# Transposing the normalised q through the DMA crossbar instead of on TensorE, in a fused linear attention and gated scan kernel

## Chip, cores, metric

One core of one Trainium2 chip. The metric is the device time of the kernel in microseconds (us). The kernel before takes 152.72 us (median of 2 runs, 152.36 to 153.08). All verdicts use runs in the fast state. By rule, a difference under 2% counts as the same; where the text calls a smaller one real, its 95% interval leaves out 1.

Names as the profile has them: PE is TensorE (matmuls), DVE the vector engine, ACT the scalar engine, POOL the GpSimd engine, SP the engine that issues the DMAs (copies between memories, done by 16 DMA engines). A lower-case name with an arrow, such as eqT<-eq, is a buffer written from another.

## The reference, cut

```python
def _attn_ref(q, k, v):                       # 8 batches, 8 heads, 576 positions, 64 wide
    q_s = np.exp(q - q.max(-1, keepdims=True)); q_s /= q_s.sum(-1, keepdims=True) + 1e-9
    k_s = np.exp(k - k.max(2, keepdims=True));  k_s /= k_s.sum(2, keepdims=True) + 1e-9
    kv = np.einsum('bhsd,bhse->bhde', k_s, v)
    return np.einsum('bhsd,bhde->bhse', q_s, kv)
# the heads side by side are x (8, 576, 512); then
    proj = x @ w_in                            # 512 -> 1024: val, gate
    h = a[0, 0] * h + val[:, t, :]             # a scan over t, kept as ys
    return (silu(gate) * ys) @ w_out           # 512 -> 512, float32
```

## The kernel before

It works on 8 batches (attention) and 9 chunks of 512 rows (projections, scan, output). Per batch: exp of q (ACT), row sums (DVE), the normalising multiplication (POOL, "norm"), exp of k (ACT), a cast of v (POOL), kv on TensorE, q transposed, xt = kv by transposed q on TensorE, and its eviction into xT (ACT). Per chunk: val and gate (TensorE), scan and gate multiplication (DVE), tanh (ACT), z (POOL), outp (TensorE), its eviction and the store.

All instructions of all engines are put in one order by a small list scheduler in the kernel. It has a cost for each operation, a "due" time for each, and rings of buffers; at each step an engine takes the operation of smallest due time among those that could start. Each engine then works strictly in this order. All DMAs are issued from SP.

```python
RINGS = {"qf": 2, "kf": 2, "vf": 2, "eq": 2, "ek": 1, "vb": 1, "eqT": 2, "kvc": 2, "y": 12,
    "th": 4, "u": 4, "z": 4, "ob": 3, "tp": 1, "ax": 1, "pp": 3, "po": 2, "qs": 3, "axp": 2, "xT": 4}
...
        def load(x, b, q2):
            ...
            nc.sync.dma_start(out=t[:, h], in_=r[:, h])          # 1152 KB: one of q, k, v of a batch
        def transp(self, e, b, g):                                # g = 0, 1, 2: 18 transposes per batch
            tp = buf("tp", (b, g))
            src = buf("eq", b).rearrange("p q c h d -> p (q c) (h d)")
            for j in range(6):
                nc.tensor.transpose(tp[:, j, :], src[:, 6 * g + j, :], ident)
        def tevac(self, e, b, g):                                 # PSUM -> SBUF on DVE or ACT
            copy(e, buf("eqT", b).rearrange("p q c h r -> p (q c) (h r)")[:, 6 * g:6 * g + 6, :],
                 buf("tp", (b, g)))
        def xt(self, e, b, q2, hf):
            xp, kvc, eqT = self._xp(b, 2 * q2 + hf), buf("kvc", b), buf("eqT", b)
            ...                                                   # rhs=eqT[r, q2, :, h2, ...]
    def idle(name, key, n):                                       # filler matmuls for the clock
        ...
        for _ in range(n):
            nc.tensor.matmul(dst, lhsT=ident, rhs=zero, start=True, stop=True)
```

The softmax here doesn't subtract the row's maximum and nothing guards it: scores larger than these inputs give would overflow.

Of the kernel before, what the change touches and what calls it, by code (L numbers as in the profile page):

```python
# [13 lines left out]
PSUM = bass.MemoryType.PSUM  # L14
# [10 lines left out]
    "cwin": {"DVE": 0.4, "POOL": 0.62, "ACT": 0.6},  # L25
# [3 lines left out]
PERIOD = 21.61  # L29
LOOK = 0.02  # L30
WARM = [0.0, 0.0]
DUE_W, DUE_CW = [-109.79, 225.14], [-179.42, 203.56]
DUE_WO, DUE_CWO, DUE_D = 501.34, -557.67, [-146.47, 373.31]
DUE = {"lq": -20.7, "lk": -40.61, "lv": -135.24, "expq": 201.96, "qsum": 161.83,
    "norm": -295.36, "expk": 15.63, "vcast": -104.69, "kv": -278.49, "transp": -215.75,
    "tevac": -180.01, "kvn": -413.4, "xt": -313.37, "xevac": -104.58, "val": -182.38,
    "scan": 210.04, "gate": -266.21, "tanh": -98.69, "gmul": -92.36, "zmul": -112.88,
    "outp": 179.81, "oevac": 92.95, "store": 182.18}
DUE_B = {
    0: {"expq": 70.47, "qsum": -5.23, "norm": 6.74, "expk": 90.41, "vcast": 61.5, "kv": 75.48,  # L40
        "transp": -244.47, "tevac": 224.73, "kvn": 118.97, "xt": -443.24, "xevac": -113.28,
        "lq": -296.19, "lk": -144.58, "lv": -63.26},
    1: {"expq": 139.16, "qsum": -170.8, "norm": -52.54, "expk": 148.63, "vcast": -144.79,
        "kv": 33.35, "tevac": -19.3, "kvn": -231.76, "xt": -7.07, "xevac": 61.09, "lq": -161.43,
        "lk": 13.79, "lv": 6.2},
}
DUE_C = {
    0: {"val": -128.64, "scan": 153.13, "gate": -14.99, "tanh": 40.59, "gmul": 85.28,
        "zmul": 191.57, "outp": -110.65, "oevac": -99.93, "store": 54.59},
    1: {"val": -73.24, "scan": -9.07, "gate": 15.05, "tanh": -32.83, "gmul": 0.37,  # L50
        "zmul": -152.72, "outp": 24.34, "oevac": -105.03, "store": -137.19},
    7: {"val": -26.9, "scan": 78.94, "gate": -10.0, "tanh": -19.5, "gmul": 166.0, "zmul": 77.14,
        "outp": -9.86, "oevac": 136.84, "store": 72.5},
    8: {"val": -5.34, "scan": 160.56, "gate": 161.01, "tanh": 107.09, "gmul": 129.49,
        "zmul": 330.75, "outp": 83.16, "oevac": 59.02, "store": -116.2},
# [3 lines left out]
       "tevac": ["DVE", "DVE", "DVE", "DVE", "DVE", "ACT"],  # L59
       "xevac": ["ACT"],  # L60
       "oevac": ["ACT", "ACT", "ACT", "DVE"],
       "norm0": ["DVE", "POOL"],
       "norm1": ["DVE", "POOL"],
       "vcast0": ["POOL", "ACT", "DVE", "POOL"],
       "xevac0": ["ACT", "DVE", "DVE", "ACT"],
       "cwin": ["ACT", "DVE", "POOL", "ACT"]}
RINGS = {"qf": 2, "kf": 2, "vf": 2, "eq": 2, "ek": 1, "vb": 1, "eqT": 2, "kvc": 2, "y": 12,
    "th": 4, "u": 4, "z": 4, "ob": 3, "tp": 1, "ax": 1, "pp": 3, "po": 2, "qs": 3, "axp": 2,
# [3 lines left out]
def operations(B, NCH, NM):  # L72
# [10 lines left out]
    for kt in range(4):  # L83
        for h in range(2):
            d = DUE_W[h] + 0.1 * kt
# [15 lines left out]
    for b in range(B):  # L101
        due = {n: PERIOD * b + x + DUE_B.get(b, {}).get(n, 0.0) for n, x in DUE.items()}
        first = b == 0
# [29 lines left out]
        for g in range(3):  # L133
            a("transp", "PE", 0.35, due["transp"] + 0.5 * g, (b, g),
              reads=[("n", b, x) for x in ((0,), (0, 1), (1,))[g]], writes=[("t", b, g)],
              uses=[("eq", b), ("tp", (b, g))])
            e, c = pick("tevac", 3 * b + g)
            a("tevac", e, c, due["tevac"] + 0.5 * g, (b, g), reads=[("t", b, g)],
              writes=[("eqT", b, g)], uses=[("tp", (b, g)), ("eqT", b)])
        a("kvn", "DVE", 0.65, due["kvn"], (b,), reads=[("kv", b)], writes=[("kvc", b)],  # L140
          uses=[("ax", ("kv", b)), ("kvc", b)])
        for h in range(4):
            key = (b, h // 2, h % 2)
            xp = "axp" if first and h != 2 else "ax"
            a("xt", "PE", COST["xt"], due["xt"] + 0.5 * h, key,
              reads=[("kvc", b), ("eqT", b, h // 2), ("eqT", b, h // 2 + 1)],
              writes=[("xp", b, h)], uses=[("kvc", b), ("eqT", b), (xp, (b, h))])
            e, c = pick("xevac0" if first else "xevac", 4 * b + h)
            a("xevac", e, c, due["xevac"] + 0.5 * h, key, reads=[("xp", b, h)],
              writes=[("xT", b)], uses=[(xp, (b, h)), ("xT", b)])  # L150
# [101 lines left out]
def kernel(  # L252
# [33 lines left out]
    for n, bufs in RINGS.items():  # L286
        if n not in ("vb", "axp", "ax", "pp", "po"):
            rings[n] = ctx.enter_context(tc.tile_pool(
                name="r_" + n, bufs=bufs, **({"space": PSUM} if n == "tp" else {})))
# [31 lines left out]

    psum["ax"] = ctx.enter_context(tc.tile_pool(name="r_ax", bufs=RINGS["ax"], space=PSUM))
    psum["warm"] = tc.alloc_tile_pool(name="r_warm", bufs=1, space=PSUM)
# [4 lines left out]
    def buf(ring, key):  # L328
        if (ring, key) not in live:
            if ring == "vb":  # L330
                live[ring, key] = vbs[key % len(vbs)]
            else:
                if ring in ("pp", "po") and ring not in psum:
                    for n in ("axp", "warm"):
                        if n in psum:
                            psum.pop(n).release()
                    psum[ring] = ctx.enter_context(tc.tile_pool(
                        name="r_" + ring, bufs=RINGS[ring], space=PSUM))
# [20 lines left out]
    class Emit:  # L359
# [62 lines left out]
        def transp(self, e, b, g):  # L422
# [3 lines left out]
            for j in range(6):  # L426
                nc.tensor.transpose(tp[:, j, :], src[:, 6 * g + j, :], ident)  # L427

# [102 lines left out]
    def idle(name, key, n):  # L531
# [6 lines left out]
        elif name == "kv":  # L538
# [50 lines left out]
```

## Time and profile before

| | before |
|---|---|
| median time | 152.72 us |
| span of the profiled run | 150.7 us |
| busy: TensorE, DVE, ACT, POOL | 125.5, 119.8, 98.5, 95.3 us |
| share of the DMA engines' span used by the loads' and stores' queue | 70.3% |
| last packet of a q, k or v load ends | 87.9 us |

The last row is read from the DMA packets of the trace: loads of q, k and v are the packets of 2304 bytes. Times are from the start of the span. The lines of the profile that matter are in the prediction.

### The profile page before, as it was taken

How to read it: one execution, taken by the hardware profiler on the slowest of the kernel's cores; microseconds unless marked ns; L12 is line 12 of the kernel's file. 1: busy time of each engine (PE TensorE's matmuls, PEld its weight loads, DVE VectorE, ACT ScalarE, POOL GpSimd, SP SyncE). 2: the span in 40 equal slices, each digit the busy share in tenths (PEclk: the TensorE clock that was granted, in tenths of full speed). 3: DMA queues.
4: the chain of work that ended last, by engine and by line, in shares of the span. 5: the costliest groups of instructions: out<-in, count | busy, mean ns of one | idle time of the engine just before them, and what ended most of it. 6: DMA issues, size and time to landing. Idle time of an engine off the chain costs nothing.

```text
span 150.7 us, 3263 instructions
## 1 busy us (share of the span) xinstructions
PE 125.5 (83%) x1293; PEld 62.6 (42%) x1312; DVE 119.8 (80%) x159; ACT 98.5 (65%) x139; POOL 95.3 (63%) x79
## 2 busy tenths in 40 slices
PE   0016559439999999999999999999999999999990
PEld 0015224312454455445445775544353444444430
DVE  0493697999899878988998997999967959995311
ACT  3616695994488899789986898597356362037450
POOL 2044029359959998994979789597950743906600
PEclk9999999965999999999999999999999999999999
DMA  4999999999999999999999970421200312042295
GB/s 163 360 395 352 331 406 411 408 408 407 412 412 412 405 408 406 407 412 412 395 409 412 406 279 30 176 77 40 100 4 0 119 59 101 7 188 92 102 373 224
DMA packets 19888, 41.11 MB, mean 273 GB/s; under 512 B 1440, under 2 KB 1440, under 8 KB 19872
## 3 DMA queue, kind: packets, MB, share of 16 engines
q1 hardware_dynamic: 19872, 40.90, 70.3%
q8 instruction: 10, 0.16, 0.4%
q14 instruction: 6, 0.05, 0.1%
HBM read 31.46 MB, written 9.44 MB: 271 GB/s over the span
## 4 chain that ended last, share of the span: by engine, by line
PE 74%; DMA 15%; ACT 5%; issue 2%; SPq 2%; DVE 1%; ACTq 0%; DVEq 0%
PE pp L479 41%; PE po L512 19%; DMA kf<-in_k_dram 15%; PE tp L427 5%; PE ax L462 5%; PE ax L440 3%; SPq L351 2%; ACT ek L398 1%; ACT eq L393 1%; PE pp L512 1%; DVE ob L357 0%; ACT eqT L355 0%; ACT ob L355 0%; ACT xT L355 0%; DVE eqT L357 0%
## 5 line engine op out<-in xcount | busy, mean ns | idle before, releaser
L479 PE MATMUL pp<-xT,win 128*128 128x512 bf16 (+1 forms) x308 | 72.4, 373 | 4.1 <-ACT xT L355 2.8
L504 POOL TENSOR_TENSOR z<-u,y 128x512 bf16<-128x512 f32 x36 | 45.0, 1272 | 22.2 <-DVE y L492 15.4
L479 PEld LDWEIGHTS <-win 128*128 128x128 bf16 x320 | 30.1, 101 | 32.5 <-issue 6.4
L492 DVE TENSOR_TENSOR_SCAN y<-decay,y,pp 128x512 f32<-128x512 f32 x32 | 39.4, 1256 | 0.2
L418 POOL TENSOR_TENSOR eq<-eq,qs 128x1152 bf16<-128x1152 bf16 x14 | 31.0, 2222 | 4.6 <-DVE qs L414 2.6
L512 PE MATMUL po<-wout,z 128*128 128x512 bf16 x129 | 32.8, 379 | 0.5 <-ACT ob L355 0.2
L497 ACT ACTIVATE th<-pp 128x512 f32<-128x512 f32 x36 | 21.4, 596 | 14.5 <-PE pp L479 14.0
L500 DVE SCALAR_TENSOR_TENSOR u<-th,pp 128x512 f32<-128x512 f32 x36 | 23.7, 674 | 5.7 <-ACT th L497 4.8
L355 ACT ACTIVATE ob<-po 128x512 f32<-128x512 f32 x26 | 15.6, 598 | 16.3 <-PE po L512 15.5
L411 DVE TENSOR_REDUCE qs<-eq 128x18 f32<-128x1152 bf16 x16 | 21.4, 1339 | 4.5 <-ACT eq L393 4.3
L357 POOL CAST vb<-vf 128x1152 bf16<-128x1152 f32 (+1 forms) x16 | 17.7, 1133 | 8.0 <-DMA vf<-in_v_dram 7.9
L427 PE MATMUL tp<-ident,eq 128*128 128x128 bf16 x144 | 13.0, 231 | 10.9 <-DVE eq L418 10.7
L393 ACT ACTIVATE eq<-qf 128x1152 bf16<-128x1152 f32 x16 | 18.5, 1161 | 4.9 <-DMA qf<-in_q_dram 4.9
L398 ACT ACTIVATE ek<-kf 128x1152 bf16<-128x1152 f32 x16 | 18.4, 1162 | 4.4 <-DMA kf<-in_k_dram 4.0
L355 ACT ACTIVATE xT<-ax 128x576 bf16<-128x576 f32 x28 | 18.2, 650 | 4.4 <-PE ax L462 4.4
L512 PEld LDWEIGHTS <-z 128*128 128x128 bf16 x144 | 13.5, 98 | 15.3 <-issue 0.4
L357 DVE COPY eqT<-tp 128x768 bf16<-128x768 bf16 x20 | 10.9, 546 | 6.6 <-PE tp L427 6.4
L427 PEld LDWEIGHTS <-eq 128*128 128x128 bf16 x144 | 9.5, 102 | 14.4 <-issue 10.9
L462 PE MATMUL ax<-eqT,kvc 64*64 64x288 bf16 x116 | 9.6, 320 | 3.3 <-ACT xT L355 1.7
L462 PEld LDWEIGHTS <-kvc 64*64 64x64 bf16 x128 | 3.8, 108 | 15.4 <-issue 12.0
L440 PE MATMUL ax<-vb,ek 64*64 64x65 bf16 x576 | 7.7, 200 | 2.1 <-ACT ek L398 1.9
L440 PEld LDWEIGHTS <-ek 64*64 64x64 bf16 x576 | 6.2, 112 | 6.2 <-ACT ek L398 3.3
(31 smaller groups left out, 49.6 us busy)
## 6 DMA issues: line engine op xcount, KB each, us to landing
out_dram<-ob SPq DMA_DIRECT2D x16, 512.0 KB, 2.9
qf<-in_q_dram SPq DMA_DIRECT2D x7, 1152.0 KB, 12.8
vf<-in_v_dram SPq DMA_DIRECT2D x7, 1152.0 KB, 11.9
kf<-in_k_dram SPq DMA_DIRECT2D x7, 1152.0 KB, 12.6
y<-in_moe_w_in_dram SPq DMA_DIRECT2D x8, 256.0 KB, 10.7
qf<-in_q_dram SPq DMA_DIRECT2D x2, 576.0 KB, 4.2
vf<-in_v_dram SPq DMA_DIRECT2D x2, 576.0 KB, 7.4
kf<-in_k_dram SPq DMA_DIRECT2D x2, 576.0 KB, 9.2
```

Source lines behind the costliest of these rows:

```text
L355: nc.scalar.activation(out, in_, AF.Copy)
L357: eng[e].tensor_copy(out, in_)
L411: nc.vector.tensor_reduce(s[:, 0].rearrange("p (a o) -> p a o", o=1), buf("eq", b)[:, q2].rearrange("p c h d -> p (c h) d"), axis=AX.X, op ...
L418: eng[e].tensor_tensor(x, x, buf("qs", (b, q2))[:, 1].rearrange("p (a o) -> p a o", o=1) .broadcast_to([128, 2 * C, D]), ALU.mult)
L427: nc.tensor.transpose(tp[:, j, :], src[:, 6 * g + j, :], ident)
L462: nc.tensor.matmul(xp[h2 * 64:h2 * 64 + 64, hp2, 0:C * n].rearrange("p (c r) -> p c r", r=n), lhsT=kvc[r, h2, q2, :], rhs=eqT[r, q2, :, h2 ...
L479: nc.tensor.matmul(dst[:, a:z], lhsT=win[:, kt, col:col + 128], rhs=xT[:, kt, s0:s0 + z - a], start=(kt == 0), stop=(kt == 3))
L492: nc.vector.tensor_tensor_scan(buf("y", (i, m)), decay[:, m, o:o + W], buf("pp", ("v", i, m)), init, op0=ALU.mult, op1=ALU.add)
L497: nc.scalar.activation(buf("th", (i, m)), buf("pp", ("g", i, m)), AF.Tanh, scale=0.5)
L500: nc.vector.scalar_tensor_tensor(buf("u", (i, m)), buf("th", (i, m)), 1.0, buf("pp", ("g", i, m)), op0=ALU.add, op1=ALU.mult)
L504: eng[e].tensor_tensor(buf("z", i)[:, m], buf("u", (i, m)), buf("y", (i, m)), ALU.mult)
L512: nc.tensor.matmul(self._po(i, r), lhsT=buf("z", i)[:, m, r * 128:(r + 1) * 128], rhs=wout[:, m], start=(m == 0), stop=(m == NM - 1))
```

## The change

The intent: relieve TensorE, which is full, of 126 of 144 transposes, and DVE of their evictions, and give the work to the DMA engines (whose transposing path is the crossbar), which have little to do after 89 us. The scheduler's constants were tuned anew with it. The core of the diff; the tables of due times are cut to what the text uses:

```diff
+    "dtransp": 2.2,                       # us of SP that the scheduler plans
-PERIOD = 21.61
-LOOK = 0.02
-WARM = [0.0, 0.0]
+PERIOD = 18.28
+LOOK = 0.06
+WARM = [3.0, 45.0]                        # filler matmuls in TensorE's planned gaps from 3 to 45 us
 ... all due times (DUE, DUE_B, DUE_C, DUE_W, DUE_CW, DUE_WO, DUE_CWO, DUE_D) and ENG are new
-RINGS: "eq": 2, "eqT": 2, "y": 12, "th": 4, "u": 4, "z": 4, "ob": 3, "po": 2
+RINGS: "eq": 3, "eqT": 3, "y": 7, "th": 2, "u": 9, "z": 3, "ob": 4, "po": 3
+        if first:
             ... transp and tevac as before ...
+        else:
+            for q2 in range(2):
+                a("dtransp", "SP", COST["dtransp"], due["transp"] + q2, (b, q2), dma=1.0,
+                  reads=[("n", b, q2)], writes=[("eqT", b, q2)], uses=[("eq", b), ("eqT", b)])
+        def dtransp(self, e, b, q2):
+            nc.sync.dma_start_transpose(
+                out=buf("eqT", b)[:, q2].rearrange("p c h r -> p c (h r)"),
+                in_=buf("eq", b)[:, q2].rearrange("p c h d -> p (c h d)"))
 (the PSUM bank of tp is freed with those of batch 0, which lets po have three)
```

More of the change, by code (lines that the diff above doesn't have):

```diff
@@ L24 @@
     "oevac": {"ACT": 0.6, "DVE": 0.68}, "kv": 0.5, "xt": 0.33,
-    "cwin": {"DVE": 0.4, "POOL": 0.62, "ACT": 0.6},
+    "dtransp": 2.2, "cwin": {"DVE": 0.4, "POOL": 0.62, "ACT": 0.6},
 }
-PERIOD = 21.61
-LOOK = 0.02
-WARM = [0.0, 0.0]
-DUE_W, DUE_CW = [-109.79, 225.14], [-179.42, 203.56]
-DUE_WO, DUE_CWO, DUE_D = 501.34, -557.67, [-146.47, 373.31]
-DUE = {"lq": -20.7, "lk": -40.61, "lv": -135.24, "expq": 201.96, "qsum": 161.83,
-    "norm": -295.36, "expk": 15.63, "vcast": -104.69, "kv": -278.49, "transp": -215.75,
-    "tevac": -180.01, "kvn": -413.4, "xt": -313.37, "xevac": -104.58, "val": -182.38,
-    "scan": 210.04, "gate": -266.21, "tanh": -98.69, "gmul": -92.36, "zmul": -112.88,
-    "outp": 179.81, "oevac": 92.95, "store": 182.18}
@@ L39 @@
-DUE_B = {
-    0: {"expq": 70.47, "qsum": -5.23, "norm": 6.74, "expk": 90.41, "vcast": 61.5, "kv": 75.48,
-        "transp": -244.47, "tevac": 224.73, "kvn": 118.97, "xt": -443.24, "xevac": -113.28,
-        "lq": -296.19, "lk": -144.58, "lv": -63.26},
-    1: {"expq": 139.16, "qsum": -170.8, "norm": -52.54, "expk": 148.63, "vcast": -144.79,
-        "kv": 33.35, "tevac": -19.3, "kvn": -231.76, "xt": -7.07, "xevac": 61.09, "lq": -161.43,
-        "lk": 13.79, "lv": 6.2},
+PERIOD = 18.28
+LOOK = 0.06
@@ new lines @@
+WARM = [3.0, 45.0]
+DUE_W, DUE_CW = [-21.84, -107.48], [176.79, -255.97]
+DUE_WO, DUE_CWO, DUE_D = 201.13, -1209.38, [177.72, 673.93]
+DUE = {"lq": -22.34, "lk": 276.5, "lv": 267.0, "expq": -91.28, "qsum": -180.34, "norm": -558.61,
+    "expk": 69.62, "vcast": -361.87, "kv": -362.46, "transp": 69.85, "tevac": 55.99,
+    "kvn": -1165.62, "xt": -468.98, "xevac": -368.08, "val": -113.19, "scan": 713.8,
+    "gate": -167.59, "tanh": -306.1, "gmul": -481.45, "zmul": 338.16, "outp": 476.71,
+    "oevac": -70.56, "store": -200.58}
@@ new lines @@
+DUE_B = {
+    0: {"expq": -228.2, "qsum": 142.64, "norm": 270.12, "expk": 414.97, "vcast": -23.61,
+        "kv": 23.55, "transp": -436.49, "tevac": 345.52, "kvn": -16.07, "xt": -524.2,
+        "xevac": 91.09, "lq": -297.9, "lk": -132.97, "lv": -169.52},
+    1: {"expq": 464.14, "qsum": -79.48, "norm": -129.84, "expk": 216.84, "vcast": -236.16,
+        "kv": -138.78, "transp": 61.35, "tevac": 11.57, "kvn": 15.55, "xt": -237.95,
+        "xevac": 21.66, "lq": -17.89, "lk": -144.35, "lv": -5.38},
@@ L46 @@
 }
 DUE_C = {
-    0: {"val": -128.64, "scan": 153.13, "gate": -14.99, "tanh": 40.59, "gmul": 85.28,
-        "zmul": 191.57, "outp": -110.65, "oevac": -99.93, "store": 54.59},
-    1: {"val": -73.24, "scan": -9.07, "gate": 15.05, "tanh": -32.83, "gmul": 0.37,
-        "zmul": -152.72, "outp": 24.34, "oevac": -105.03, "store": -137.19},
-    7: {"val": -26.9, "scan": 78.94, "gate": -10.0, "tanh": -19.5, "gmul": 166.0, "zmul": 77.14,
-        "outp": -9.86, "oevac": 136.84, "store": 72.5},
-    8: {"val": -5.34, "scan": 160.56, "gate": 161.01, "tanh": 107.09, "gmul": 129.49,
-        "zmul": 330.75, "outp": 83.16, "oevac": 59.02, "store": -116.2},
+    0: {"val": -161.1, "scan": 376.05, "gate": 145.05, "tanh": -20.67, "gmul": 17.53,
+        "zmul": 310.65, "outp": -168.86, "oevac": 72.02, "store": -237.11},
@@ L56 @@
+    1: {"val": -135.84, "scan": -146.88, "gate": -80.64, "tanh": -129.49, "gmul": 216.18,
+        "zmul": -164.46, "outp": -55.68, "oevac": -425.21, "store": -257.66},
+    7: {"val": -240.68, "scan": 454.02, "gate": -178.32, "tanh": 16.59, "gmul": 371.24,
+        "zmul": 39.76, "outp": 85.5, "oevac": 10.19, "store": 67.9},
+    8: {"val": -245.31, "scan": -100.08, "gate": -63.52, "tanh": -83.48, "gmul": 42.52,
+        "zmul": 214.48, "outp": 140.71, "oevac": -199.0, "store": -33.8},
 }
@@ L58 @@
        "vcast": ["POOL"],
-       "tevac": ["DVE", "DVE", "DVE", "DVE", "DVE", "ACT"],
+       "tevac": ["DVE", "ACT", "DVE"],
        "xevac": ["ACT"],
        "oevac": ["ACT", "ACT", "ACT", "DVE"],
-       "norm0": ["DVE", "POOL"],
-       "norm1": ["DVE", "POOL"],
-       "vcast0": ["POOL", "ACT", "DVE", "POOL"],
+       "norm0": ["POOL", "DVE"],
+       "norm1": ["POOL"],
+       "vcast0": ["POOL", "ACT", "DVE", "ACT"],
        "xevac0": ["ACT", "DVE", "DVE", "ACT"],
        "cwin": ["ACT", "DVE", "POOL", "ACT"]}
-RINGS = {"qf": 2, "kf": 2, "vf": 2, "eq": 2, "ek": 1, "vb": 1, "eqT": 2, "kvc": 2, "y": 12,
-    "th": 4, "u": 4, "z": 4, "ob": 3, "tp": 1, "ax": 1, "pp": 3, "po": 2, "qs": 3, "axp": 2,
+RINGS = {"qf": 2, "kf": 2, "vf": 2, "eq": 3, "ek": 1, "vb": 1, "eqT": 3, "kvc": 2, "y": 7,
+    "th": 2, "u": 9, "z": 3, "ob": 4, "tp": 1, "ax": 1, "pp": 3, "po": 3, "qs": 3, "axp": 2,
     "xT": 4}
@@ L132, in operations @@
               uses=[("ek", b), ("vb", b), ("ax", ("kv", b))])
-        for g in range(3):
-            a("transp", "PE", 0.35, due["transp"] + 0.5 * g, (b, g),
-              reads=[("n", b, x) for x in ((0,), (0, 1), (1,))[g]], writes=[("t", b, g)],
-              uses=[("eq", b), ("tp", (b, g))])
-            e, c = pick("tevac", 3 * b + g)
-            a("tevac", e, c, due["tevac"] + 0.5 * g, (b, g), reads=[("t", b, g)],
-              writes=[("eqT", b, g)], uses=[("tp", (b, g)), ("eqT", b)])
+        if first:
+            for g in range(3):
+                a("transp", "PE", 0.35, due["transp"] + 0.5 * g, (b, g),
+                  reads=[("n", b, x) for x in ((0,), (0, 1), (1,))[g]], writes=[("t", b, g)],
+                  uses=[("eq", b), ("tp", (b, g))])
+                e, c = pick("tevac", g)
+                a("tevac", e, c, due["tevac"] + 0.5 * g, (b, g), reads=[("t", b, g)],
+                  writes=[("eqT", b, q2) for q2 in range(2) if g in (q2, q2 + 1)],
+                  uses=[("tp", (b, g)), ("eqT", b)])
+        else:
+            for q2 in range(2):
+                a("dtransp", "SP", COST["dtransp"], due["transp"] + q2, (b, q2), dma=1.0,
+                  reads=[("n", b, q2)], writes=[("eqT", b, q2)], uses=[("eq", b), ("eqT", b)])
         a("kvn", "DVE", 0.65, due["kvn"], (b,), reads=[("kv", b)], writes=[("kvc", b)],
@@ L145, in operations @@
             a("xt", "PE", COST["xt"], due["xt"] + 0.5 * h, key,
-              reads=[("kvc", b), ("eqT", b, h // 2), ("eqT", b, h // 2 + 1)],
+              reads=[("kvc", b), ("eqT", b, h // 2)],
               writes=[("xp", b, h)], uses=[("kvc", b), ("eqT", b), (xp, (b, h))])
@@ L286 @@
     for n, bufs in RINGS.items():
-        if n not in ("vb", "axp", "ax", "pp", "po"):
-            rings[n] = ctx.enter_context(tc.tile_pool(
-                name="r_" + n, bufs=bufs, **({"space": PSUM} if n == "tp" else {})))
+        if n not in ("vb", "tp", "axp", "ax", "pp", "po"):
+            rings[n] = ctx.enter_context(tc.tile_pool(name="r_" + n, bufs=bufs))
     psum = {}
@@ L322 @@
     psum["ax"] = ctx.enter_context(tc.tile_pool(name="r_ax", bufs=RINGS["ax"], space=PSUM))
+    psum["tp"] = tc.alloc_tile_pool(name="r_tp", bufs=RINGS["tp"], space=PSUM)
     psum["warm"] = tc.alloc_tile_pool(name="r_warm", bufs=1, space=PSUM)
@@ L333, in buf @@
                 if ring in ("pp", "po") and ring not in psum:
-                    for n in ("axp", "warm"):
+                    for n in ("axp", "warm", "tp"):
                         if n in psum:
@@ L537, in idle @@
             dst = emit._po(*key)
-        elif name == "kv":
+        elif name == "kv" and ("ax", ("kv", key[0])) not in live:
             dst = buf("ax", ("kv", key[0]))[:, 0]
```

## The prediction

> **What bounds the kernel now.** I read the page's busy shares and slices first, then the busy time in windows, then the chain in order of time, then the groups. The slices are 3.77 us each:
>
> ```profile
> PE 125.5 (83%) x1293; PEld 62.6 (42%) x1312; DVE 119.8 (80%) x159; ACT 98.5 (65%) x139; POOL 95.3 (63%) x79
> PE   0016559439999999999999999999999999999990
> PEclk9999999965999999999999999999999999999999
> DMA  4999999999999999999999970421200312042295
> GB/s 163 360 395 352 331 406 411 408 408 407 412 412 412 405 408 406 407 412 412 395 409 412 406 279 30 176 77 40 100 4 0 119 59 101 7 188 92 102 373 224
> ```
>
> There are two stages. Until about 35 us PE works half the time and the DMA engines are full; from there to the end PE is at 9 in each slice. The DMA engines stay full to slice 24 (about 89 us), when the last input has landed, and then have some 60 us with little to do. The windows say it in us:
>
> ```profile
> 30.00:45.00 15.00, 12.21 (x112) 5.43 (x118) 14.15 (x17) 10.28 (x17) 11.55 (x8) 0.77 1.04 410
> 60.00:75.00 15.00, 14.89 (x163) 7.01 (x163) 13.91 (x21) 13.29 (x20) 12.61 (x9) 1.00 1.04 406
> 75.00:90.00 15.00, 14.89 (x188) 9.47 (x190) 14.15 (x21) 12.38 (x19) 12.23 (x9) 1.00 0.99 386
> ```
>
> The columns are PE, PEld, DVE, ACT, POOL, clock, DMA share, GB/s. PE is busy 14.89 of 15 us, DVE 13.9 to 14.2, so DVE is the second bound, close behind. "Busy" could flatter a pipelined engine, so I checked the chain: 16 projection matmuls of 512 columns take 3.45 us, 216 ns each, again and again. PE really has no room after 39 us. The chain also shows the transposes and a slow piece:
>
> ```profile
> 35.17 3.34 PE pp L479 x8
> 38.76 0.44 PE tp L427 x6
> 39.20 3.45 PE pp L479 x16
> 42.65 0.34 PE tp L427 x6
> ```
>
> The same eight matmuls take 3.34 us (417 ns each) at 35 us and 1.73 us later: this is the dip to 0.77 of the clock in the window 30 to 45. The groups concerned, and the chain by line:
>
> ```profile
> L427 PE MATMUL tp<-ident,eq 128*128 128x128 bf16 x144 | 13.0, 231 | 10.9 <-DVE eq L418 10.7
> L357 DVE COPY eqT<-tp 128x768 bf16<-128x768 bf16 x20 | 10.9, 546 | 6.6 <-PE tp L427 6.4
> L355 ACT ACTIVATE eqT<-tp 128x768 bf16<-128x768 bf16 x4 | 3.3, 814 | 0.0
> PE pp L479 41%; PE po L512 19%; DMA kf<-in_k_dram 15%; PE tp L427 5%; PE ax L462 5%; PE ax L440 3%; SPq L351 2%; ACT ek L398 1%; ACT eq L393 1%; PE pp L512 1%; DVE ob L357 0%; ACT eqT L355 0%; ACT ob L355 0%; ACT xT L355 0%; DVE eqT L357 0%
> ```
>
> A transpose counts 231 ns busy, but six of them hold the chain for 0.34 to 0.44 us: the chain's length, not the busy time, is what can be saved.
>
> **What the Trainium skill says.** (1) "VectorE: DVE Perf Modes", section on the three transpose paths: a 128x128 bf16 transpose takes 390 ns on TensorE and ends in PSUM, 1309 ns through the DMA crossbar and ends in SBUF. The trace puts TensorE's at 231 ns alone and some 70 ns in a row of six; it has no DMA transpose. (2) "DMA: Bandwidth & Descriptors", section "Latency and other measured facts": a DMA transpose moves 261 GB/s in a bad layout, 350 to 400 in a contiguous one. The kernel before can't show it; its plain loads move 405 to 412. (3) The same page, section "Queues, rings and completion order": the DMAs from SP have one ring on each DMA engine, consumed in order. The trace agrees in that a load of 1152 KB takes 12.6 us from issue to landing though its bytes need 2.9 us at 408 GB/s: it stands behind others. A transpose will stand there too. (4) "TensorE: Matmul & The Clock Gate", Part 1: after an idle window of about 3.4 us the PE clock halves. The trace agrees: around PE's gaps at 29 to 33 us the matmuls go from 216 to 417 ns.
>
> **The change part by part.**
>
> *Removed from PE.* 7 of 8 batches lose their 18 transposes, 126 of 144. The chain gives the transpose line 4.9% of 150.7 us = 7.4 us; the pieces listed are 16 of 0.34 to 0.49 us, all after 38 us, thus batches 2 to 7 and on the path. The transposes of batch 1 (25 to 28 us) lie where PE waits anyway. Gain 7.4 us, full size only if PE stays the bound.
>
> *Removed from DVE and ACT.* 21 of 24 evictions. The 24 are 20 on DVE and 4 on ACT; with one ACT and two DVE left for batch 0, DVE loses 18 x 0.546 = 9.8 us, ACT 3 x 0.814 = 2.4 us. Per batch DVE then has 4 scans x 1.256 + 4 x 0.674 + 2 x (1.339 + 0.266) + 0.6 for kv's norm + 0.7 = 12.2 us in place of some 13.5. PE has per batch 48 x 0.216 = 10.4 for the projections, 0.8 for kv, 1.3 for xt: 12.5. So PE remains the bound by a hair, and the removal from DVE doesn't count twice. It is needed so that DVE doesn't take over.
>
> *Added to DMA.* 14 transposes of 128 x 1152 bf16 = 0.295 MB, 4.13 MB in all. At 261 GB/s (estimate from the skill's figure) 1.13 us each, 15.8 us together. The last input lands at 89 + 16 = 105 us if the DMA engines stay full. Chunk 7 of the projections needs batch 7. Two chunks are 2 x 10.4 = 21 us, so it starts 23 to 25 us before the end, about 118 us if the end is at 142. From the last k to the first projection batch 0 takes 7.5 us in the trace (ek at 12.89, pp at 20.40). 105 + 7.5 = 112.5 is before 118: hidden, with little to spare.
>
> *Added to SP.* The diff plans 2.2 us of SP for each: 31 us of an engine that otherwise issues loads at 0.4 to 0.5 us each. It is in order: a transpose that waits for its norm holds the loads behind it. I take a loss of some bubbles for it, below.
>
> *Moved: the order of loads.* SP takes the smallest due time among what can be issued. Before, the second half of w_in goes out at 17.5 to 22.6 us, behind batch 1's q, v and k; the gate matmuls start at 33.3. In the diff w_in's second half has -107, q of batch 1 -22, the first half -22, v of batch 0 98 and k of batch 0 143. So q0, w_in (7 of 8 pieces fit the ring), q1, v0, k0 come first: 1.18 + 1.05 + 1.18 + 0.79 + 1.18 + 1.18 = 6.56 MB. With the rates of the first six slices this has landed at 20 us, against k0 at about 13 us before. Batch 0's attention ends later, first projection about 25 us instead of 20.4, but val and gate can go on without the hole at 28 to 33 us. At 33.3 us the kernel before had done 16 val matmuls (3.5 us) and batch 1's kv (0.8); the new one may have done 8 us. Gain up to 4 us.
>
> *Filler matmuls until 45 us.* They keep the clock up where the model sees gaps. The cold stretch from 33.3 to 38.4 us cost 1.6 us on the eight matmuls and 0.4 on those before: gain 2 us, if the gaps aren't filled by the new order anyway.
>
> *Rings.* po grows to 3, eq and eqT to 3, y shrinks to 7; PE lost only 0.5 us on po waits, so I give these nothing.
>
> Sum: 152.7 - 7.4 - 4 - 2 = 139.3. Against it I set 4.2 us: the four engines are then within 10% of each other (PE 12.5, DVE 12.2, POOL 4 x 1.27 + 2 x 2.22 + 2 x 1.18 = 11.9), and an in-order kernel with all of them that full loses a few per cent; and the transposes land late at times. Prediction 143.5 us.
>
> **The rivals.** *The wait moves into xt.* A transpose stands up to 12 us behind loads, and xt waits for it where it waited 0.3 us for an eviction. For it: the 12.6 us to landing, and SP blocked behind norms. Against it: eq and eqT have three buffers, and the old kernel has a backlog of projections for PE (its attention ends at 118 us, 30 us before the end). If xt starved PE 0.6 us a batch and the new start gave nothing, 147 to 149 us.
>
> *DMA becomes the bound.* If a transpose holds all DMA engines for 2.5 us or more, 35 us are added, the last input lands at 124, and the end is 124 + 7.5 + 23 = 154 or later; at 4 us each beyond 170. For it: the DMA is full until 89 us; the 1309 ns for one block, times nine blocks, would be 11.8 us if blocks didn't overlap. Against it: the skill's 261 GB/s, and the diff's plan of 1.0 us.
>
> *Only PE's work counts.* The start is bounded by the same bytes and the new order brings nothing: 152.7 - 7.4 = 145.3.
>
> **Range and chances.** The best case is the sum without the loss and a better start, 137; the rival with starved xt gives 149, so 137 to 150.5 should hold 8 times in 10. Slower needs the DMA-bound rival, to which I give 6%; within 2% (149.7 to 155.8) needs most of the gains lost, 12%; faster 82%.
>
> **What would show it.** Right: PE still 9 in each slice after 30 us and no cold clock there; 18 transposes left; DVE busy about 110 us; DMA transposes of about 1 to 1.5 us of engine time each, inputs all landed near 105 us; first gate matmul before 30 us. Wrong: gaps of PE before xt with a DMA as the releaser; DMA share at 1 beyond 115 us; SP waits on POOL's norm with DMA below 400 GB/s in the first 90 us; DVE fuller than PE.

## The result, and the profile after

The changed kernel takes 162.52 us (162.1 to 162.95) against 152.72: ratio 1.0642, 95% interval 1.0481 to 1.0803. It is slower; the interval is wide, for each kernel had two runs. Ratios in this document are the mean time of one kernel's fast runs over that of the other's of the same rounds, so not quite the ratio of the medians quoted.

The page of the changed kernel, busy shares and slices of 4.03 us, two groups and the DMA issues:

```profile
PE 142.1 (88%) x1289; PEld 63.9 (40%) x1289; DVE 108.8 (68%) x140; ACT 97.1 (60%) x137; POOL 95.1 (59%) x79
PE   6977999786789999998699989479999999999991
DMA  5899999999999999999999999999996006030096
GB/s 182 275 409 410 410 411 384 412 305 217 406 368 221 391 386 162 319 408 213 374 410 409 254 291 349 187 338 407 229 380 265 0 9 251 0 130 4 38 358 258
...
L557 PE MATMUL warm<-zero,ident 128*128 128x512 bf16 x81 | 21.1, 412 | 1.4 <-POOL ident masks.py:199 1.4
...
eqT<-eq SPq DMA_TRANSPOSE x14, 8.9
```

TensorE's 142.1 us contain 21 us of fillers. DVE fell by 11 us, near the 9.8 worked out. The DMA engines are full to slice 30, about 121 us, where they were full to 89; but their rate falls again and again from 410 to between 160 and 300 GB/s. The last packet of a load ends at 115.1 us in place of 87.9. The chain of the changed kernel, in order of time, runs through loads of q from 37 to 76 us (three of its pieces):

```profile
37.22 11.69 DMA qf<-in_q_dram
...
50.17 12.48 DMA qf<-in_q_dram
...
64.04 12.27 DMA qf<-in_q_dram
```

Each is issued when the one before has landed and been used: 13 to 14.5 us a batch. TensorE needs about 13.8: the prediction's 12.5 counts the 48 projection and output matmuls of a chunk, but nine chunks fall on eight batches, so it is 54 x 0.216 + 0.8 + 1.3. The loads thus no longer run ahead of TensorE. From 76 to 93 us the chain goes through the engines, and from 93.6 to 104.6 through a load of k. TensorE, which had 14.89 of 15 us in the windows from 60 us before, now has gaps:

```profile
75.00:90.00 15.00, 13.79 (x185) 7.03 (x185) 11.55 (x16) 11.53 (x17) 11.62 (x9) 1.00 1.00 367
90.00:105.00 15.00, 11.68 (x86) 6.75 (x84) 11.30 (x15) 7.59 (x12) 11.45 (x9) 1.00 1.12 259
```

One pair of transposes close up, in windows of 1 us (the last two columns are the DMA share and GB/s):

```profile
33.00:34.00 1.00, 1.00 (x5) 0.41 (x5) 1.00 (x2) 1.00 (x2) 0.72 (x2) 1.00 1.04 408
34.00:35.00 1.00, 1.00 (x6) 0.49 (x5) 1.00 (x2) 1.00 (x2) 1.00 (x3) 1.00 1.65 290
35.00:36.00 1.00, 1.00 (x40) 0.48 (x38) 1.00 (x2) 0.10 (x2) 1.00 (x3) 1.00 0.82 142
36.00:37.00 1.00, 1.00 (x32) 0.42 (x33) 0.82 (x1) 1.00 (x1) 1.00 (x2) 1.00 1.34 272
37.00:38.00 1.00, 1.00 (x36) 0.45 (x24) 0.65 (x3) 0.16 (x1) 1.00 (x1) 1.00 2.20 96
38.00:39.00 1.00, 0.69 (x7) 0.30 (x6) 1.00 (x1) 0.73 (x2) 1.00 (x2) 1.00 0.38 102
```

For 5 us, from 34 to 39, the engines move 0.90 MB in all, 0.59 MB of it the two transposes. At 408 GB/s 5 us are 2.04 MB. The loads thus lost 1.73 MB or 4.2 us to this pair; it is one of the dearer ones. The DMA view of 33 to 40 us, GB/s in slots of 0.175 us, shows a standstill:

```profile
GB/s 421 421 421 408 408 363 373 353 279 262 215 155 135 86 48 123 284 287 276 288 287 171 322 276 227 9 0 0 6 7 10 9 15 352 408 369 263 421 408 421
```

From 37.4 to 38.8 us almost nothing moves, though SP had issued the next loads of v and k at 36.12 and 36.67 us. In the packets of the trace (a transpose's have 256 bytes) transposes are in flight in all that time, and no packet of a load starts between 35.5 and 38.8 us. Summed up to the last load, the transposes' packets hold the 16 engines for 24.4 us (their time in flight, at most 16 at once): 12.4 transposes, 2.0 us each. For 8.0 of these us less than 50 GB/s move. From 5 us to the last load, packets of some kind keep the engines busy but for 1.2 us in all, so the engines were not left without work by a late issue.

### The profile page after: what moved, and what is told of

Its sections match the earlier page's. It is cut to its first block, busy times and chain, and to the rows that moved or that the text cites. A ratio compares the mean times of both kernels' runs of the same rounds, so it can differ in the third digit from the quotient of the medians.

```text
span 161.1 us, 3246 instructions
## 1 busy us (share of the span) xinstructions
PE 142.1 (88%) x1289; PEld 63.9 (40%) x1289; DVE 108.8 (68%) x140; ACT 97.1 (60%) x137; POOL 95.1 (59%) x79
## 4 chain that ended last, share of the span: by engine, by line
DMA 42%; PE 37%; ACT 8%; DVE 4%; issue 4%; SPq 2%; POOL 2%; ACTq 0%; POOLq 0%
DMA qf<-in_q_dram 35%; PE pp L491 21%; PE po L524 12%; DMA kf<-in_k_dram 7%; ACT th L509 3%; ACT eq L399 2%; PE ax L474 2%; POOL vb L363 1%; PE ax L452 1%; DVE y L504 1%; DVE u L512 1%; SPq L357 1%; ACT ek L404 1%; SPq L376 1%; PE pp L524 1%
## 5 line engine op out<-in xcount | busy, mean ns | idle before, releaser
L491 PE MATMUL pp<-xT,win 128*128 128x512 bf16 (+1 forms) x320 | 70.7, 367 | 1.2 <-DVE u L512 1.1
L424 POOL TENSOR_TENSOR eq<-eq,qs 128x1152 bf16<-128x1152 bf16 x15 | 32.1, 2149 | 18.2 <-DVE qs L420 13.4
L491 PEld LDWEIGHTS <-win 128*128 128x128 bf16 x320 | 29.4, 99 | 33.2 <-issue 5.7
L363 POOL CAST vb<-vf 128x1152 bf16<-128x1152 f32 (+1 forms) x15 | 16.5, 1116 | 10.0 <-DMA vf<-in_v_dram 7.7
L557 PE MATMUL warm<-zero,ident 128*128 128x512 bf16 x81 | 21.1, 412 | 1.4 <-POOL ident masks.py:199 1.4
L557 PEld LDWEIGHTS <-ident 128*128 128x128 bf16 x103 | 10.0, 103 | 16.8 <-issue 6.5
L363 DVE COPY ob<-po 128x512 f32<-128x512 f32 x8 | 5.4, 673 | 6.9 <-PE po L524 6.9
L474 PEld LDWEIGHTS <-kvc 64*64 64x64 bf16 x128 | 3.8, 103 | 13.8 <-issue 12.5
## 6 DMA issues: line engine op xcount, KB each, us to landing
qf<-in_q_dram SPq DMA_DIRECT2D x7, 1152.0 KB, 11.9
```

The lines of the kernel that those rows point to most:

```text
L363: eng[e].tensor_copy(out, in_)
L424: eng[e].tensor_tensor(x, x, buf("qs", (b, q2))[:, 1].rearrange("p (a o) -> p a o", o=1) .broadcast_to([128, 2 * C, D]), ALU.mult)
L491: nc.tensor.matmul(dst[:, a:z], lhsT=win[:, kt, col:col + 128], rhs=xT[:, kt, s0:s0 + z - a], start=(kt == 0), stop=(kt == 3))
```

## The experiments

Three theories were set up. E: the transposes take the DMA engines from the loads. Q: SP, which works in order, waits for norms and issues the loads behind them late. O: the new order, rings and fillers cost the time, whatever transposes. Seventeen kernels ran; an eighteenth did not build. Runs marked "wrong on purpose" read the untransposed q; the comparison with the reference passed all of them, so it is too coarse here to tell whether q is transposed, and it vouches no more for the transposes of the changed kernel.

### The changed order with less and less of a transpose

**No transpose at all** (wrong on purpose):

```diff
         def dtransp(self, e, b, q2):
-            nc.sync.dma_start_transpose(...)
+            pass
-            xp, kvc, eqT = ..., buf("eqT", b)            # in xt
+            xp, kvc, eqT = ..., buf("eq" if b else "eqT", b)
```

> The changed kernel in its own order, with no transpose at all (wrong result on purpose: xt reads the untransposed eq). Three theories for the 162.5 us. Theory E (engines): each DMA transpose takes the 16 DMA engines about 2.5 us, 14 of them 35 us. Theory Q (queue): SP waits in order for POOL's norm, and the loads behind it are issued late. Theory O (order): the new order of instructions, rings and filler matmuls cost the time, whatever transposes. E and Q expect 138 to 145 us here, with the last input landed near 90 us; O expects 155 us or more.

155.31 us (one of the four runs was slow and is left out), ratio 1.0188 (1.0111 to 1.0266); the last load packet ends at 92.3 us. So a part of the loss is not the transposes': with no transpose anywhere this order is still slower than the kernel before, as O said.

**A 4 KB copy in its place** (wrong on purpose):

```diff
-            nc.sync.dma_start_transpose(out=...[:, q2]..., in_=...)
+            nc.sync.dma_start(out=...[:, 0:16], in_=...[:, 0:16])     # same waits; xt reads eq
```

> The changed kernel in its own order; in the place of each transpose SP issues a copy of 4 KB from eq to eqT with the same waits (wrong result on purpose: xt reads eq). E expects the time of the run without transposes, within 2 us; Q expects most of the loss, 155 us or more, with SP's waits on POOL still some 60 us in total; O expects no difference from the run without transposes.

154.24 us, ratio 1.0157 (1.0087 to 1.0228). SP's waits for norms, 21.9 us of them in this run's trace, cost nothing: Q, in its form of waiting for norms, has fallen.

**A plain copy of the full size** (wrong on purpose):

```diff
-            nc.sync.dma_start_transpose(out=... "p c h r -> p c (h r)", in_=...)
+            nc.sync.dma_start(out=... "p c h r -> p (c h r)", in_=...)
```

> The changed kernel in its own order, each transpose replaced by a plain copy of the same 295 KB from eq to eqT (wrong result on purpose), so that xt waits for the DMA as before. If what costs the engines is the crossbar (E), the copies cost 0.7 us each, 10 us of DMA in all, and the time is within 4 us of the run with 4 KB copies, 140 to 149 us; if bytes or the place in the ring behind loads are what costs, 155 us or more; Q expects 157 to 163.

155.11 us, ratio 1.0188 (1.0124 to 1.0252), as with none. The bytes, the place in the queue and xt's wait for a DMA are free (E's 140 to 149 missed, for it left out the order's share). What the transposes add, 162.5 - 155.3 = 7.2 us, belongs to transposing.

**TensorE's transposes put back into this order:**

```diff
-            nc.sync.dma_start_transpose(...)
+            for g in ((0,), (1, 2))[q2]:       # six nc.tensor.transpose, then nc.vector.tensor_copy
+                ...                            # po has 2 buffers
```

> The changed kernel in its own order, but each DMA transpose is put back on TensorE at the same place of the order (with the evictions on VectorE; po gets two buffers, since the transposes need their PSUM bank). The result is right. E and Q expect 145 to 152 us: TensorE's 7 to 9 us back, the loads landed near 90 us. O expects 158 us or more.

172.11 us, ratio 1.1361 (1.1269 to 1.1452). E's and Q's 145 to 152 missed. O's "158 or more" held, but O does not explain a time 17 us above the same order without transposes. The order was made for transposes that cost TensorE and DVE nothing, and these engines may now wait for them at places that don't suit (DVE stands 14.1 us for TensorE's transposes). It shows that an exact undoing in a fixed order is no fair control here, nothing more.

### The transposes in the old order

**The crossbar in the kernel before**, its order kept:

```diff
         def transp(self, e, b, g):
+            if b:
+                if g != 1:
+                    nc.sync.dma_start_transpose(out=buf("eqT", b)[:, g // 2]..., in_=buf("eq", b)[:, g // 2]...)
+                return
         def tevac(self, e, b, g):
+            if b:
+                return
```

> The kernel before in its own order, rings and due times; only the transposes of batches 1 to 7 go through the crossbar, issued from SP at the place of the order where TensorE's stood. The runs so far: the changed kernel's order without any transpose is 1.9% slower than the kernel before, and the transposes add about 7 us to that. If the new order is what costs (O), the transposes alone are worth having here: 145 to 150 us. If the transposes cost the DMA some 7 us net in any order (E), 153 to 160 us, with the last input landed at 110 us or later.

173.19 us, ratio 1.1369 (1.1325 to 1.1414): 21 us lost in the old order, more than both theories expected. From its waits:

```profile
PE ax L470 <- DMA eqT<-eq: 23.0, 4, 15.1
```

TensorE stands 23 us in four waits of xt for a transpose, 15.1 in one. The rival that the wait moves into xt is real where the order isn't made for it; in the changed kernel this wait is 0.9 us.

**No transposes in the old order** (wrong on purpose). The first try did not build (a deadlock over eq's two buffers):

> The kernel before in its own order without the transposes and evictions of batches 1 to 7 (wrong result on purpose: xt reads the untransposed eq). This is the gain to be had if transposing were free. My step that takes 7.4 us off the path expects 144 to 146 us; if VectorE, POOL or the loads hold TensorE as soon as it is relieved, 148 us or more.

With a third eq buffer:

```diff
         def transp(self, e, b, g):
+            if b:
+                return                        # tevac likewise; xt reads eq
-                name="r_" + n, bufs=bufs, ...
+                name="r_" + n, bufs=3 if n == "eq" else bufs, ...
```

> The kernel before in its own order without the transposes and evictions of batches 1 to 7 (wrong result on purpose: xt reads the untransposed eq, whose pool gets a third buffer, without which the order deadlocks). This is what free transposing is worth in the old order. My step that takes 7.4 us off the path expects 144 to 146 us; if the loads, VectorE or POOL hold TensorE as soon as it is relieved, 148 us or more.

146.6 us, ratio 0.964 (0.9599 to 0.9681). Free transposing is worth 5.4 us in the old order (a third eq buffer included, whose own worth no run shows). My 7.4 us were a third too many, but the step was sound.

**Idle transposes beside the kernel before.** This separates their cost from everything that waits for them:

```diff
+    dsrc, dum = ...                           # a constant tile, two scratch tiles [128, 1152] bf16
         def transp(self, e, b, g):
+            if b and g != 1:
+                nc.sync.dma_start_transpose(out=dum[g // 2]..., in_=dsrc)
             tp = buf("tp", (b, g))            # TensorE's transposes as before
```

> The kernel before as it is, with its transposes on TensorE, plus 14 idle DMA transposes of the same size from a constant tile to a scratch tile, issued on SP at two places per batch. Nothing waits for them except the next write of the scratch tile, and they wait for no norm. Shows what they cost the loads. E expects the last input to land at 100 us or later in place of 89, and the time up by 1 to 8 us; Q expects the time within 1 us of the kernel before.

165.61 us, ratio 1.0899 (1.0845 to 1.0953): 13.2 us lost to transposes whose result nobody reads, and which wait for no norm. SP, and two of the waits of the whole run:

```profile
29.87 7.20 SPq L429 DMA_TRANSPOSE dum<-dsrc  x1
37.17 1.87 SPq L354 DMA_DIRECT2D vf<-in_v_dram  x1
39.10 3.82 SPq L429 DMA_TRANSPOSE dum<-dsrc  x1
...
POOL vb L360 <- DMA vf<-in_v_dram: 13.7, 3, 6.5
...
ACT ob L358 <- DMA out_dram<-ob: 8.5, 3, 5.3
```

SP is held 3 to 7 us by each up to 100 us, and loads and stores stand behind. POOL waits 13.7 us for v (7.9 in the kernel before), ACT 8.5 us for a store to give an output buffer back (no such wait before). How much of the 13.2 us is due to late loads and how much to late stores, no run tells. The last load packet ends at 103.2 us, 15.3 us later than in the kernel before. By SP's list nine idle transposes were issued before 95 us, so they took some 1.7 us each from the loads; by the packets, 8.4 of them had run and held the engines for 16.8 us, 2.0 each, of which less than 50 GB/s moved in 5.8. And note 103.2: this is earlier than the 105 us that the prediction called hidden.

**The same with idle copies:**

```diff
-                nc.sync.dma_start_transpose(out=dum[g // 2]..., in_=dsrc)
+                nc.sync.dma_start(out=dum[g // 2], in_=dsrc)
```

> As dummy_in_before, but the 14 idle transfers of 295 KB are plain copies, not transposes. The transposes cost 13 us. If it is the crossbar's rate and its small packets that cost the loads, the copies cost at most 4 us and the loads land before 97 us; if it is any transfer that SP puts among the loads, 10 us or more.

152.74 us, ratio 1.0035 (1.0001 to 1.0069). The same bytes at the same places cost half a microsecond, at most 1. The crossbar is what costs.

**A row of transposes alone**, after the last store:

```diff
+    for i in range(8):
+        nc.sync.dma_start_transpose(out=xT[...]..., in_=w)      # w: 1152 columns of win
+    for i in range(8):
+        nc.sync.dma_start(out=xT[...], in_=w)
```

> The kernel before, and after its last store 8 DMA transposes of 128x1152 bf16 from one SBUF tile into 8 places of another, with no wait between them, then 8 plain copies of the same size into the same places. The cost by itself, no load beside it. From the packets of the changed kernel a transpose runs at about 285 GB/s, 1.03 us: 8 in about 8.5 us plus 2 us to land if the engines limit; 24 us if SP's issue (3.0 us at the least in the changed kernel) limits. The copies: 8 in about 6 us.

```profile
148.10 11.14 SPq L561 DMA_TRANSPOSE xT<-win  x8
159.30 5.15 SPq L564 DMA_DIRECT2D xT<-win  x8
```

169.07 us with these sixteen transfers. SP spends 11.14 / 8 = 1.39 us on a transpose and 0.64 on a copy; by the packets the eight transposes take 11.0 us and the eight copies 6.0. The DMA view of 148 to 168 us (GB/s, slots of 0.5 us; transposes from 149.4 to 160.4) shows what the 1.39 us are made of:

```profile
GB/s 270 381 174 287 268 69 289 236 116 290 185 178 290 126 259 288 64 284 277 79 291 226 131 290 170 309 392 438 378 433 382 429 396 419 415 396 332 0 0 0
```

A transpose moves at some 290 GB/s, 1.03 us, and between two there is a gap. Its packets hold the engines for 1.05 us, as expected, and the stretches under 50 GB/s within them add up to 0.05 us for all eight. The 3.0 us for SP did not show. So a transpose by itself costs the engines what the prediction said, and among loads twice that.

**Loads from ScalarE instead of SP**, a control, and with the idle transposes on SP:

```diff
-        nc.sync.dma_start(out=t[:, h], in_=r[:, h])
+        (nc.scalar if b > 1 else nc.sync).dma_start(out=t[:, h], in_=r[:, h])
```

> The kernel before, but the loads of batches 2 to 7 are issued from ScalarE instead of SP, at the same places of the order. A control for the next run: 151 to 157 us, ScalarE pays about 0.4 us for each of 18 loads and may wait in order for a buffer.

> The last kernel plus the 14 idle DMA transposes on SP of the run dummy_in_before, where they cost 13 us. There SP was held 3.3 to 7.2 us by each, though they waited for no norm and a row of 8 alone took 1.4 us each. If the loss is that SP is held, and loads behind it are issued late, then loads from another engine lose little: at most 5 us over the control. If the engines themselves stand still for a transpose among loads, the loss stays at 8 us or more over the control.

165.98 us (ratio 1.0886, 1.0821 to 1.0951) and 166.64 us (1.0933, 1.0872 to 1.0994). The idle transposes cost under 1 us over the control. That would fit "SP held", but the control is itself 14 us slow (151 to 157 had been expected) and its DMA engines are at 5 to 8 tenths in several slices, so transposes may fall into holes. The pair doesn't decide whether it is SP's being held or the engines' standing still that stops the loads. The packets do, for the changed kernel and for the idle transposes: up to the last load the engines are short of packets for 1.2 and 0.7 us in all, and held by transposes for 24.4 and 16.8. It is the engines. Why packets stand among loads, and whether SP is held because they stand, no run shows.

### The order

**The fillers off in the changed kernel:**

```diff
-WARM = [3.0, 45.0]
+WARM = [0.0, 0.0]
```

> The changed kernel without its filler matmuls; order and transposes as they are, the result right. My prediction gave the fillers 2 us of gain. In the trace they stand on the path: between 38 and 47 us each xt of batch 1 waits behind 3 to 8 fillers into the same PSUM buffer, some 4 us in all. If the fillers cost, 158 to 160 us and the first matmuls of chunk 1 near 43 us instead of 46.8; if the warm clock is worth more, 163 us or more.

162.9 us, ratio 1.0646 (1.055 to 1.0741): no change, between the two times expected.

**The fillers off, and no transposes** (wrong on purpose; both edits above):

> The changed kernel's order without any transpose (wrong result on purpose) and without the fillers. With fillers it was 1.9% slower than the kernel before. If the fillers make the hole at the start, 150 to 152 us; if the loss is elsewhere in the order, 154 us or more.

152.44 us, ratio 1.0008 (0.9982 to 1.0034) against 1.0188 with fillers. So the fillers cost 2% where loads don't bind, and nothing where they do, which fits the loads hiding them. How they cost, from TensorE's timeline in the run without transposes (L472 is xt, L555 the filler):

```profile
38.35 0.32 PE L472 MATMUL ax<-eq,kvc 64*64 64x288 bf16 x4
40.48 1.89 PE L555 MATMUL ax<-zero,ident 128*128 128x512 bf16 x7 [1.81 <-ACT xT L361]
42.30 0.32 PE L472 MATMUL ax<-eq,kvc 64*64 64x288 bf16 x4
43.37 0.81 PE L555 MATMUL ax<-zero,ident 128*128 128x512 bf16 x3 [0.75 <-ACT xT L361]
```

They write to the one buffer ax, so they wait for the eviction like xt itself and then stand ahead of it. Chunk 1 starts at 46.8 us; without fillers at 43.9.

**The fillers on in the kernel before:**

```diff
-WARM = [0.0, 0.0]
+WARM = [3.0, 45.0]
```

> The kernel before with the fillers of the change switched on (3 to 45 us of the scheduler's time), nothing else. My prediction's term was 2 us of gain, from the cold stretch at 33 to 38 us: 150 to 151 us. If the fillers get in the way of real work as in the changed kernel, 153 us or more.

152.95 us, ratio 1.0032 (1.0004 to 1.0059), with a mean granted clock of 1.0 against 0.977 in the profiled runs. The cold stretch is gone and the time isn't: the eight gate matmuls that took 3.41 us at 35.1 us take 1.90, but xt of batch 1 stands behind eight fillers into ax, so the first gate matmul comes at 34.98 us instead of 33.30, and chunk 1 starts at 38.6 instead of 39.0. The clock's gain was there, and the fillers' own delay took it back.

**What is left of the order.** Without fillers and transposes the new order takes the time of the kernel before; the old order without transposes takes 5.4 us less. Busy time to 35, to 47 and to 90 us, for the kernel before and then for the new order without fillers and transposes:

```profile
0.00:35.00 35.00, 15.24 (x226) 8.16 (x228) 24.62 (x34) 22.35 (x26) 13.83 (x21) 0.95 0.96 361
35.00:47.00 12.00, 11.58 (x132) 5.57 (x130) 11.21 (x16) 8.52 (x12) 10.37 (x8) 0.87 1.04 410
47.00:90.00 43.00, 42.52 (x495) 22.59 (x502) 39.09 (x57) 37.22 (x55) 37.66 (x27) 1.00 1.02 400
```

```profile
0.00:35.00 35.00, 12.00 (x129) 6.46 (x130) 21.34 (x29) 21.64 (x26) 13.49 (x17) 1.00 0.98 368
35.00:47.00 12.00, 7.67 (x107) 3.12 (x105) 9.05 (x12) 9.10 (x11) 11.99 (x12) 0.86 1.04 410
47.00:90.00 43.00, 43.00 (x521) 20.28 (x520) 37.55 (x53) 35.82 (x52) 36.74 (x27) 1.00 1.01 377
```

By 47 us the kernel before has issued 56 projection matmuls' weights and kv of three batches, the new order 41 and two. The like comparison is with the old order without transposes, whose trace has 60 and three: 19 x 0.216 + 0.8 = 4.9 us of work. After that TensorE is full in both (42.99 and 43.00 of 43 us to 90). So most of the 5.4 us are lost in the start. Two runs went after the cause. The first moved the decay rates ahead, behind which POOL's cast of v waits (edits on top of the last one):

```diff
+    # in the scheduler's order: lalog first, the four decay before expq of batch 1
+    order = order[:at] + dec + order[at:]
```

> As l0_warm0 (the changed order, no transposes, no fillers; wrong result on purpose), but the decay rates are loaded first and their four exponentials stand ahead of batch 1's exp of q on ScalarE. In the trace POOL's cast of batch 1's v stands behind the settings of decay, which wait for ScalarE to 35 us, and kv of batch 1 starts at 36.3 us. If that in-order wait makes the hole before chunk 1, kv starts near 33 us and the time falls by 2 to 3 us, to 149.5 to 150.5 us; if batch 1's v itself is what comes late, less than 1 us.

152.53 us, ratio 1.0002 (0.9978 to 1.0026): nothing. POOL's cast then waited for the load itself:

```profile
33.68 2.24 POOL L363 CAST vb<-vf 128x1152 bf16<-128x1152 f32 x2 [0.91 <-DMA vf<-in_v_dram]
```

So batch 1's v is cast 8 us later than in the kernel before, where this cast runs at 25.5. The second run moved it:

```diff
+    put(("lv", 1, None), ("lq", 2, None)); put(("lk", 1, None), ("lq", 2, None))
+    # vcast, expk, kv, kvn, xt, xevac of batch 1 moved up on their engines as well
```

> As l0_decay_early (no transposes, no fillers; wrong result on purpose), which brought nothing: there POOL's cast of batch 1's v waited for the load of v to 33.7 us, against 25.5 us in the kernel before. Here v and k of batch 1 are loaded ahead of q of batch 2, the last piece of w_in and w_out; the cast, the exp of k, kv, xt and its eviction of batch 1 move up on their engines in the same measure. If late loads of batch 1 make the hole before chunk 1, its first matmul comes at 38 to 41 us in place of 43.6 and the time falls by 2 to 5 us, to 147.5 to 150.5 us. If the time stays at 152, the loss lies elsewhere in the order.

159.79 us, ratio 1.0499 (1.0426 to 1.0571), the opposite of what I expected. ScalarE's timeline says why:

```profile
30.41 1.16 ACT L399 ACTIVATE eq<-qf 128x1152 bf16<-128x1152 f32 x1 [8.72 <-DMA qf<-in_q_dram]
```

The exp of batch 2's q stands ahead of the eviction of batch 0's xT on ScalarE. With q of batch 2 loaded later, ScalarE waits 8.72 us and the first projection starts at 33.8 us instead of 27. The exp of batch 2's q came 6.8 us later than in the run before (30.4 against 23.6), and the kernel took 7.3 us more. The run leaves open what the best order of loads would be worth; it shows how tightly the in-order queues tie the time to each load.

### Transposes only after the loads

If the transposes cost only among loads, they should be put where there are none. Batches 6 and 7 alone, in the kernel before:

```diff
+        if b not in (6, 7):
             ... transp, tevac as before ...
+        else:
+            ... dtransp, as in the change ...
```

> The kernel before with the crossbar for batches 6 and 7 alone, whose q is normalised when nearly all loads have landed; all else as before (its list scheduler sets the order again). If the transposes cost by delaying loads, these four cost nothing and TensorE saves 36 transposes, 2.5 us: 149 to 151 us. If a transpose costs its latency wherever it stands, 153 us or more.

150.08 us, ratio 0.9884 (0.9819 to 0.9949): 1.2% faster than the kernel before (under the 2% that a verdict asks for, but the interval leaves out 1), 7.7% under the changed one. The scheduler set the order anew here, so a part of the gain may be the order's; no control without these four transposes was run. SP's time per transpose, first in this kernel, then in the changed one (ns, min/median/max):

```profile
L439 SPq DMA_TRANSPOSE eqT<-eq x4: 1283/1344/1457, 88.7 to 103.7; - x4
```

```profile
L437 SPq DMA_TRANSPOSE eqT<-eq x14: 3005/4652/8085, 25.2 to 113.9; - x14
```

The same instruction holds SP for 1.3 us where no loads are in flight and for 4.7 us among loads. The time to land falls from 8.9 to 3.2 us. (The figures of the changed kernel include waits for a norm; those of the idle transposes, 3.3 to 7.2 us, do not.)

## Why the prediction was wrong, point by point

- **TensorE's gain.** Right in mechanism. 7.4 us were mis-sized: 5.4 us measured in the old order. The costs per batch (12.5 for TensorE, 12.2, 11.9) mix up batch and chunk: work of the projections, the scan and the output comes nine times, not eight, and TensorE's is 13.8. The other engines' costs grow with it, so TensorE stays the bound by a hair.
- **The transposes' own cost.** 1.13 us of the engines each is right with nothing beside it (1.05) and too little among loads. In the changed kernel the last load packet ends 22.8 us later than in the same order without transposes (115.1 against 92.3), with 13 issued by then: 1.75 us each, or 2.0 by the packets. I had expected 105.
- **"Hidden, with little to spare": the step that failed.** I asked only when the last batch must have landed, and found 105 + 7.5 before 118. The overlap was wrong: late loads in the middle cost time at once. The idle transposes show it with nothing else changed: the last load at 103.2 us, within my limit, and 13.2 us lost, with engines waiting for loads and stores in between. In the changed kernel TensorE has 13.79 and 11.68 of 15 us from 75 and from 90 us, and the transposes cost 7.2 us. The reason that fits is the fixed order: attention and projections stand in fixed places on each engine, and the engines can't draw on the projections in hand while one of them waits for a load or a store. The idle DMA engines after 89 us were not slack for the loads before it.
- **SP.** I took 2.2 us each from the diff and bubbles as part of a 4.2 us reserve. SP is held 3.0 to 8.1 us. Waiting for norms, which I named as the danger, costs nothing (4 KB copies).
- **"Gain up to 4 us" from the order of loads.** The first gate matmul did come before 30 us, as predicted (first projection at 27.1, first tanh of a gate at 28.2). But batch 1's v comes 8 us later for it, and the new order without fillers and transposes gives nothing where the old order without transposes gives 5.4. This step is of the wrong sign by that much; most of it (4.9 us of TensorE's work) lies before 47 us. Which change of the order causes it stays open: the two runs that tried one cause each did not find it.
- **Fillers, 2 us.** The clock's part was right (eight matmuls in 1.90 us in place of 3.41). What it left out is that fillers delay the work behind them: nothing gained in the old order, 2% lost in the new order where loads don't bind. (The dip itself agrees with a window of 3.4 idle us only in the halving: PE's gaps before it are 1.5 and 1.7 us, with 0.3 us of matmuls between.)
- **The rivals.** "DMA becomes the bound" was the right one, at 6%. It needed 2.5 us per transpose in my account; 2.0 were enough, since it isn't the last load alone that counts. It put the end at 154 us or later; 162.5 came.

The sum as the runs give it, without fillers, which the loads hide: 152.4 (kernel before) - 5.4 (no transposing in the old order) + 5.4 (new order, back to 152.4) + 10.5 (transposes, to 162.9 in the changed kernel without fillers). With fillers the last term splits into 2.9 for fillers and 7.2 for transposes. What stays open: why the engines stand still for part of a transpose among loads; and the cause within the order's 5.4 us.

## What to carry to other kernels

An engine that is idle on average is no place to move work to if it is full in the stage where the work arises; measure the moved work by itself with idle copies of it (a run with the results unused) before building the change. In a kernel whose engines all run in one fixed order, slack at the end of a queue need not be slack in its middle: ask of each load, not of the last alone, what waits for it. Put crossbar transposes where no loads are in flight, and don't let clock fillers write to a buffer that real work waits for.

## What the Trainium skill lacked or had wrong

- "Advanced Engine Details and Errata", section "X-Bar Transpose (TRN2)", says that transpose DMAs are as fast as regular ones. Here, SBUF to SBUF, 128x1152 bf16, both in rows of 8: 1.38 us against 0.75 us for a plain copy by the packets.
- "DMA: Bandwidth & Descriptors", section "Latency and other measured facts", gives 261 GB/s, 350 to 400 in the contiguous case. Measured alone: some 290 GB/s while the packets move, 212 with the gaps of a row. Among loads the engines are held 2.0 us for 0.295 MB, about 150 GB/s.
- No page says that a transpose among loads keeps the engines with packets that don't move: less than 50 GB/s in 8.0 of 24.4 us in the changed kernel, in 0.05 of 8.4 us in a row alone.
- No page says that a transpose holds the engine that issues it much longer among other transfers: 1.3 to 1.4 us alone, 3.3 to 7.2 us among loads with no wait of its own, so that what is queued behind it is issued late.
- No page speaks of filler matmuls that keep the clock up, or of their price: mean clock 1.0 against 0.977, eight matmuls in 1.90 us against 3.41, and the time up by 0.3%.
